# First MLP's weight conversion: ScalarE writes the scaled absolute value into a tile of its own

## The chip, the cores and the metric

The kernel runs on one core of a Trainium2 chip. The core has five instruction queues: TensorE (PE, matrix products), VectorE (DVE), ScalarE (ACT), GpSimd (POOL) and SyncE (SP, which here only issues DMA transfers). Each queue runs its own instructions in the order in which they stand; between queues, an instruction waits for semaphores. The metric is device microseconds (us) of the program. Before the change three runs took 1099.03, 1103.13 and 1106.37 us; their median is 1103.13 us.

## What is computed

Attention with a decay bias over 4 batches, 8 heads, 576 positions and 64 dimensions, and then two MLPs over the 2304 rows of its output, all to nearly float32 exactness. The weights come as float64.

```python
scores = where(causal, -1e9, q @ k.T / 8 + minimum(-(cum[:, None] - cum[None, :]), 0))   # cum = cumsum(relu(s))
attn   = softmax(scores) ; x = attn @ v                    # then (2304, 512)
h = x @ w_in ; g = relu(h) + log1p(exp(-abs(h))) ; x1 = g @ w_out      # first MLP,  512 -> 2048 -> 512
h = x1 @ w_in2 ; g = P(h) / (Q(h) + 1e-6) ; out = g @ w_out2           # second MLP, same sizes
```

## The kernel before

**Products.** Each float32 operand is split into a high part (rounded to the type that PE multiplies at full rate) and a low part (the rest), and a product is three matmuls: high by high, high by low, low by high.

**Tiles.** The first MLP goes over tiles of rows: T0 and T1 of 256 rows each, then four of 448. For each of 16 slices `ff` of the hidden dimension a *unit* multiplies the rows with the slice of `w_in` (`stage_a`, lines 670 to 672, into bank `h`), applies the activation (`stage1`, lines 760 to 764: three ACT instructions and one DVE; `stage3`, lines 800 and 802: high part on ACT, low part on POOL) and multiplies with the slice of `w_out` (`stage_b`, lines 706 to 708, into `acc`). The units run T0 with `ff` 0 to 7, T1 with `ff` 0 to 7, then T0 and T1 in turn for `ff` 8 to 15, then the tiles of 448. Attention is interleaved with the units: scores (L318, L319), softmax (L299 to L315), transposes (L372 to L392) with their split (L362, L363), and the product with `v` (L418 to L430).

**Weights.** The float64 words of the first MLP's weights are loaded as pairs of 32-bit words, 512 KB for each of 32 halves (`load_w`, L519 to L521), and turned into float32 on the chip. This is *a conversion*; it makes a tile `tc` (two buffers), in `conv_t`: POOL makes a zero that has the sign of the high word (L536), ACT scales the high word's absolute value in place (L537), DVE shifts the word that ACT wrote and ORs it to POOL's result (L538), and ORs the top bits of the low word to that (L543). Then `conv_hl` makes the high part `w1h` on ACT (L547) and the low part `w1l` on POOL (L548), and a DMA keeps `w1l` in DRAM. L537 writes the same word that L536 reads, so ACT waits for POOL, and DVE waits for ACT. A loaded buffer is free for the next load when L543 has read it. 7 conversions stand before the first unit, the other 25 beside the units of T0 and T1. From the tiles of 448 rows on none of the first MLP's is left; their `w1l` is loaded back.

**Rows of the activations.** `split_x` (L639 on ACT, L640 on DVE) makes the high and low part of the 512 columns of a tile of rows in four steps `k`, in tiles with the tag `xs`: nine buffers of 128x512 words for the whole kernel. T0 and T1 take four each (high and low share one), a tile of 448 rows two for each `k`.

**Order.** A scheduler writes each engine's order when the program is built, from its own estimate of when operands are ready, priorities (`ahead`, `early`) and some fixed orders (`queue_behind`). An edit of one instruction can so move many others.

Of the kernel before, what the change touches and what calls it, by code (L numbers as in the profile page):

```python
# [8 lines left out]
F32 = mybir.dt.float32  # L9
F32R = mybir.dt.float32r  # L10
I32 = mybir.dt.int32
AF = mybir.ActivationFunctionType
ALU = mybir.AluOpType
# [41 lines left out]
def moe_chain_kernel(ctx, tc, qk0, qk, vv, s0, s, w1, w2, ab, out):  # L55
    nc = tc.nc
    sb = ctx.enter_context(tc.tile_pool(name="sb", bufs=1))
# [466 lines left out]
    def conv(m, ff, half, hi, lo):  # L524
        conv_hl(conv_t(m, ff, half), hi, lo)

    def conv_t(m, ff, half):
        r = raw64.pop((m, ff, half))
        lw = r[:, :, 0]
        hf = r.bitcast(F32)[:, :, 1]  # L530
        hw = r[:, :, 1]
        t = sb.tile([128, 512], F32, tag="tc", bufs=2, name="tc")
        ti = t.bitcast(I32)
        if m == 0:

            nc.gpsimd.tensor_scalar(t, hf, 0.0, 1.0, op0=ALU.mult, op1=ALU.mult)  # L536
            nc.scalar.activation(hf, hf, AF.Abs, scale=2.0 ** -112)  # L537
            nc.vector.scalar_tensor_tensor(ti, hw, 3, ti, op0=ALU.logical_shift_left, op1=ALU.bitwise_or)  # L538
        else:
            nc.gpsimd.tensor_scalar(hf, hf, 2.0 ** -112, 1.0, op0=ALU.mult, op1=ALU.mult)  # L540
            nc.vector.tensor_scalar(ti, hw, 3, None, op0=ALU.logical_shift_left)
            nc.vector.scalar_tensor_tensor(ti, hw, -2147483648, ti, op0=ALU.bitwise_and, op1=ALU.bitwise_or)
        nc.vector.scalar_tensor_tensor(ti, lw, 29, ti, op0=ALU.logical_shift_right, op1=ALU.bitwise_or)  # L543
        return t
# [29 lines left out]
    def conv2_a(ff, half):  # L574
        c2_open.append((ff, half, conv_t(1, ff, half)))
# [476 lines left out]
```

## Time and profile before

| what | value |
|---|---|
| three runs, us | 1099.03, 1103.13, 1106.37 |
| span of the profiled execution, us | 1100.2 |
| busy: PE, DVE, ACT, POOL, us | 1030.3, 825.4, 836.6, 488.2 |
| first matmul of a tile of 448 rows begins at, us | 240.9 |
| PE busy before 241 us, and from 241 to 1100 us | 184.8 of 241, 845.5 of 859 |

The profile gives the span of the profiled execution, from its first to its last instruction, and no other time of it; the span lies between the lowest and the median of the three runs. Rows of the trace name the line of the kernel, the engine, the tile that is written and the tiles read; `[1.97 <-POOL tc L536]` behind a row says that the engine stood idle for 1.97 us before it, until that instruction of POOL. In a table of stretches (windows) the columns are the stretch, its length, and then for PE, PEld (loading of weights into PE), DVE, ACT and POOL the busy time and, in brackets, the number of instructions; then TensorE's granted clock as a share of full speed, the share of the DMA engines' time, and GB/s. In a list of waits each row gives the waiting engine and line, whom it waited for, the sum in us, how often, and the longest.

### The profile page before, as it was taken

The numbers are of one execution on the slowest core, as the hardware profiler recorded it, in microseconds if no ns is written. First come the engines' busy times: TensorE is split into PE (matmuls) and PEld (weight loads), VectorE is DVE, ScalarE is ACT, GpSimd is POOL, SyncE is SP. The second block draws the span as 40 slices with busy tenths as digits, with TensorE's granted clock in tenths as the row PEclk, the third lists the DMA queues.
The fourth block names the chain that finished last, engine by engine and source line by source line (L and its number), as shares of the span: only waits on it lengthen the run. The fifth ranks groups of instructions, "written<-read, shape, count | busy, mean of one in ns | idle before, by whom it ended". The sixth has DMA issues, their size and how long they took to land.

```text
span 1100.2 us, 17835 instructions
## 1 busy us (share of the span) xinstructions
PE 1030.3 (94%) x5732; PEld 926.5 (84%) x5732; DVE 825.4 (75%) x1904; ACT 836.6 (76%) x1767; POOL 488.2 (44%) x543
## 2 busy tenths in 40 slices
PE   3588889889999999999999999899999999999998
PEld 3477778789888888888999998799999999999996
DVE  6898998777888788886556677667777677776765
ACT  6698888878787788777556555688788888888885
POOL 3655576552222122221244676445445455454543
PEclk9999999999999999999999999899999999999999
DMA  6464566466555464432777974401000010000000
GB/s 227 167 221 158 181 222 217 162 205 178 166 160 158 142 205 132 154 94 66 226 235 223 323 280 149 160 1 45 13 30 29 1 58 1 29 30 1 30 1 29
DMA packets 70493, 140.53 MB, mean 128 GB/s; under 512 B 8384, under 2 KB 23904, under 8 KB 70400
## 3 DMA queue, kind: packets, MB, share of 16 engines
q1 hardware_dynamic: 68000, 135.37, 37.5%
q10 hardware_dynamic: 2400, 4.03, 1.5%
q8 instruction: 45, 0.74, 0.3%
q14 instruction: 48, 0.39, 0.1%
HBM read 112.66 MB, written 22.61 MB: 123 GB/s over the span
## 4 chain that ended last, share of the span: by engine, by line
PE 65%; DVE 5%; DMA 3%; ACT 3%; POOL 2%; issue 2%; SPq 0%; POOLq 0%; ACTq 0%; DVEq 0%
PE h L672 6%; PE h L671 6%; PE h L670 6%; PE acc L715 6%; PE acc L714 6%; PE acc L713 6%; PE at L418 3%; PE at L670 3%; PE at L672 3%; PE at L671 3%; PE acc L706 3%; PE acc L707 3%; PE acc L708 3%; PE at L318 2%; DMA raw64x<-in_w_dram 2%
## 5 line engine op out<-in xcount | busy, mean ns | idle before, releaser
L671 PE MATMUL h<-xs,w1h 128*128 128x448 f32 (+1 forms) x352 | 119.9, 341 | 1.4 <-DVE xs L640 1.4
L670 PE MATMUL h<-xs,w1h 128*128 128x448 f32 (+1 forms) x352 | 119.9, 342 | 1.3 <-DVE e L764 1.0
L707 PE MATMUL acc<-gl,w1h 128*128 128x448 f32 (+1 forms) x352 | 119.1, 338 | 1.2 <-POOL gl L802 1.2
L706 PE MATMUL acc<-gh,w1h 128*128 128x448 f32 (+1 forms) x352 | 119.7, 341 | 0.1
L672 PE MATMUL h<-xs,w1l 128*128 128x448 f32 (+1 forms) x352 | 118.8, 338 | 0.2 <-POOL w1l L548 0.2
L708 PE MATMUL acc<-gh,w1l 128*128 128x448 f32 (+1 forms) x352 | 118.4, 336 | 0.0
L715 PE MATMUL acc<-w2h,gl 128*128 128x512 f32 x288 | 113.8, 395 | 0.4 <-POOL gl L802 0.4
L713 PE MATMUL acc<-w2h,gh 128*128 128x512 f32 x288 | 113.8, 395 | 0.4 <-ACT gh L800 0.4
L714 PE MATMUL acc<-w2l,gh 128*128 128x512 f32 x288 | 113.6, 394 | 0.0
L315 POOL TENSOR_SCALAR PA<-PA,stat 128x384 f32<-128x384 f32 (+3 forms) x112 | 69.3, 622 | 97.2 <-DVE stat L314 51.9
L802 POOL TENSOR_TENSOR gl<-PA,gh 128x384 fp32r<-128x384 f32 x96 | 99.4, 1036 | 6.3 <-issue 4.0
L773 POOL TENSOR_TENSOR tc<-tc,e 128x384 f32<-128x384 f32 x48 | 51.7, 1076 | 102.7 <-ACT tc L771 102.7
L315 POOL TENSOR_SCALAR P<-P,stat 128x576 f32<-128x576 f32 x32 | 26.2, 819 | 143.2 <-DVE stat L313 50.7
L363 DVE TENSOR_TENSOR ptl<-at,pth 128x384 fp32r<-128x384 f32 (+2 forms) x108 | 60.7, 569 | 16.3 <-ACT pth L362 15.1
L312 ACT ACTIVATE PA<-PA,stat 128x384 f32<-128x384 f32 (+3 forms) x112 | 63.9, 571 | 10.3 <-DVE stat L299 9.0
L670 PEld LDWEIGHTS h<-xs,w1h 128*128 128x128 f32 x352 | 67.0, 191 | 5.5 <-DVE e L764 1.7
L671 PEld LDWEIGHTS h<-xs,w1h 128*128 128x128 f32 x352 | 66.8, 190 | 5.0 <-DVE xs L640 2.2
L707 PEld LDWEIGHTS acc<-gl,w1h 128*128 128x128 f32 x352 | 66.4, 189 | 4.9 <-POOL gl L802 2.0
L362 ACT ACTIVATE pth<-at 128x384 fp32r<-128x384 f32 (+2 forms) x108 | 53.3, 499 | 21.4 <-PE at L392 12.2
L706 PEld LDWEIGHTS acc<-gh,w1h 128*128 128x128 f32 x352 | 66.4, 189 | 3.6 <-DVE yb L736 0.5
L672 PEld LDWEIGHTS h<-xs,w1l 128*128 128x128 f32 x352 | 66.6, 189 | 3.1 <-POOL w1l L548 0.4
L708 PEld LDWEIGHTS acc<-gh,w1l 128*128 128x128 f32 x352 | 66.2, 188 | 3.0
(225 smaller groups left out, 3311.9 us busy)
## 6 DMA issues: line engine op xcount, KB each, us to landing
w1l<-l_d SPq DMA_DIRECT2D x148, 256.0 KB
raw<-in_w_dram SPq DMA_DIRECT2D x48, 512.0 KB
raw<-in_qk_dram SPq DMA_DIRECT2D x32, 384.0 KB
l_d<-w1l SPq DMA_DIRECT2D x32, 256.0 KB
raw64x<-in_w_dram SPq DMA_DIRECT2D x16, 512.0 KB
R<-in_vv_dram SPq DMA_DIRECT2D x16, 320.0 KB
raw<-in_qk_dram SPq DMA_DIRECT2D x8, 576.0 KB
out_dram<-yb SPq DMA_DIRECT2D x18, 256.0 KB
```

What stands on the lines that cost most here:

```text
L312: nc.scalar.activation(pt[:, 0:n], pt[:, 0:n], AF.Exp, bias=mn, scale=-1.0, accum_out=stat[:, i, 1:2])
L315: nc.gpsimd.tensor_scalar(pt[:, 0:n], pt[:, 0:n], stat[:, i, 2:3], 1.0, op0=ALU.mult, op1=ALU.mult)
L670: nc.tensor.matmul(h, wh[:, cs], xh, start=(k == 0), stop=False)
L671: nc.tensor.matmul(h, wh[:, cs], xl, start=False, stop=False)
L672: nc.tensor.matmul(h, wl[:, cs], xh, start=False, stop=(k == KD - 1))
L706: nc.tensor.matmul(o, wh[:, cs], gh, start=first and not both, stop=False)
L707: nc.tensor.matmul(o, wh[:, cs], gl, start=False, stop=False)
L708: nc.tensor.matmul(o, wl[:, cs], gh, start=False, stop=last and (not both or m % 2 == 1))
L713: nc.tensor.matmul(acc[m], gh[:, cs], wh, start=first, stop=False)
L714: nc.tensor.matmul(acc[m], gh[:, cs], wl, start=False, stop=False)
L715: nc.tensor.matmul(acc[m], gl[:, cs], wh, start=False, stop=last)
L802: eng.tensor_tensor(gl, g, f(gh), op=ALU.subtract)
```

## The change

ACT's instruction writes a tile `xa` of its own, and DVE reads that tile in place of the loaded word. `xa` is taken from the nine `xs` buffers. No instruction is added or removed; line numbers behind it go up by two.

```diff
             nc.gpsimd.tensor_scalar(t, hf, 0.0, 1.0, op0=ALU.mult, op1=ALU.mult)
-            nc.scalar.activation(hf, hf, AF.Abs, scale=2.0 ** -112)
-            nc.vector.scalar_tensor_tensor(ti, hw, 3, ti, op0=ALU.logical_shift_left, op1=ALU.bitwise_or)
+            a = sb.tile([128, 512], F32, tag="xs", bufs=9, name="xa")
+            nc.scalar.activation(a, hf, AF.Abs, scale=2.0 ** -112)
+            nc.vector.scalar_tensor_tensor(
+                ti, a.bitcast(I32), 3, ti, op0=ALU.logical_shift_left, op1=ALU.bitwise_or)
```

The scheduler's order changes on all engines up to the start of the tiles of 448 rows, and hardly behind it. Three places:

ACT, in the attention of the first heads, around the third and fourth conversion (`raw_395`, `raw_397` are their loaded words; `pth` is the high part of a head's transposed probabilities, `gh` the probabilities). Before:

```order
L312 ACTIVATE gh,stat<-gh,stat 128x256 [waits DVE_49]
L537 ACTIVATE raw_395<-raw_395 128x512 [waits DMAHW4_49,Pool_49]
L362 ACTIVATE pth<-acc 128x384 [waits PE_49]
L537 ACTIVATE raw_397<-raw_397 128x512 [waits DMAHW5_49,Pool_49]
L312 ACTIVATE gh,stat<-gh,stat 128x128 [waits DVE_49]
```

With the change:

```order
L538 ACTIVATE xa<-raw_395 128x512 [waits DMAHW4_49]
L312 ACTIVATE gh,stat<-gh,stat 128x128 [waits DVE_49,Pool_49]
L290 ACTIVATE vs<-R 128x5x2x64 [waits DMAHW2_49]
L549 ACTIVATE w1h<-tc 128x512 [waits DVE_49]
L281 ACTIVATE st<-raw 64x576 [waits DMAHW5_49]
L549 ACTIVATE w1h<-tc 128x512 [waits DVE_49,Pool_49]
L312 ACTIVATE gh,stat<-gh,stat 128x256 [waits DVE_49]
L362 ACTIVATE pth<-acc 128x384 [waits PE_49]
L312 ACTIVATE gh,stat<-gh,stat 128x128 [waits DVE_49,Pool_49]
L538 ACTIVATE xa<-raw_397 128x512 [waits DMAHW7_49]
```

The conversion's instruction waits for its load alone, no longer for POOL, and stands further ahead: the third one six rows ahead of the `pth` that it stood directly in front of.

ACT, at the end of T1, behind the last conversion (`xs<-x_277 128x64` and `xs<-x_1873 128x384` are the high parts of one `k` of the first tile of 448 rows). Before, in whose order the first `k` stands more than 100 rows further up:

```order
L537 ACTIVATE raw_2948<-raw_2948 128x512 [waits DMAHW3_49,Pool_49]
L800 ACTIVATE gh<-e 128x256 [waits DVE_49]
L761 ACTIVATE e<-e 128x256 [waits Activation_49]
L290 ACTIVATE vs<-R 128x5x2x64 [waits DMAHW1_49]
L762 ACTIVATE e<-e 128x256 [waits Activation_49]
L547 ACTIVATE w1h<-tc 128x512 [waits DVE_49]
L760 ACTIVATE e<-h 128x256 [waits PE_49,Pool_49]
L639 ACTIVATE xs<-x_277 128x64
L800 ACTIVATE gh<-e 128x256 [waits DVE_49]
L761 ACTIVATE e<-e 128x256 [waits Activation_49]
L639 ACTIVATE xs<-x_1873 128x384
```

With the change:

```order
L538 ACTIVATE xa<-raw_2976 128x512 [waits DMAHW3_49]
L764 ACTIVATE e<-e 128x256 [waits Activation_49]
L762 ACTIVATE e<-h 128x256 [waits PE_49,Pool_49]
L290 ACTIVATE vs<-R 128x5x2x64 [waits DMAHW0_49]
L802 ACTIVATE gh<-e 128x256 [waits DVE_49]
L763 ACTIVATE e<-e 128x256 [waits Activation_49]
L549 ACTIVATE w1h<-tc 128x512 [waits DVE_49]
L764 ACTIVATE e<-e 128x256 [waits Activation_49]
L641 ACTIVATE xs<-x_277 128x64
L641 ACTIVATE xs<-x_1890 128x384
```

All four `k` now stand behind the last conversion, three did before: the ninth buffer, which took the first `k` early, now goes from conversion to conversion.

PE, where attention of the first rows ends and the first unit begins (`at<-ht` and `acc<-ht` are scores of the next rows, `h<-xs,w1h` the first unit). Before:

```order
L318 MATMUL at<-ht 128x384 [waits DVE_49,PE_49,Activation_49]
L319 MATMUL at<-st 128x384 [waits DMAHW4_49]
L418 MATMUL h<-pth,vs_285 128x256 [waits Activation_49]
L418 MATMUL h<-pth,vs_285 128x256
L372 MATMUL acc<-ident,gh 128x128 [waits PE_49,Pool_49]
L372 MATMUL acc<-ident,gh 128x128 x2
L318 MATMUL acc<-ht 128x512 [waits PE_49]
L319 MATMUL acc<-st 128x512
```

With the change:

```order
L418 MATMUL h<-pth,vs_285 128x256 [waits Activation_49]
L418 MATMUL h<-pth,vs_285 128x256
L418 MATMUL h<-ptl,vs_285 128x256 [waits DVE_49]
L418 MATMUL h<-ptl,vs_285 128x256
L672 MATMUL h<-xs,w1h 128x256 [waits PE_49,Activation_49]
L318 MATMUL at<-ht 128x384 [waits DVE_49]
L319 MATMUL at<-st 128x384 [waits DMAHW5_49]
L318 MATMUL acc<-ht 128x512
```

The last head's product with `v` and one matmul of the first unit now stand ahead of the next scores.

## Rows read from the trace of the kernel before

**Rows 1.** The page: span, and busy time with its share and instructions by engine.

```profile
span 1100.2 us, 17835 instructions
PE 1030.3 (94%) x5732; PEld 926.5 (84%) x5732; DVE 825.4 (75%) x1904; ACT 836.6 (76%) x1767; POOL 488.2 (44%) x543
```

**Rows 2.** Windows by stage; columns as told above.

```profile
0.00:57.00 57.00, 27.74 (x103) 22.65 (x103) 42.66 (x128) 37.67 (x88) 29.09 (x46) 1.00 0.59 199
57.00:120.00 63.00, 52.82 (x367) 47.02 (x365) 56.41 (x155) 54.73 (x130) 36.07 (x41) 0.97 0.52 176
120.00:178.00 58.00, 51.02 (x383) 46.71 (x383) 52.93 (x147) 51.53 (x138) 36.49 (x47) 1.00 0.68 223
178.00:241.00 63.00, 53.25 (x417) 50.80 (x416) 49.11 (x116) 50.28 (x128) 39.31 (x45) 1.00 0.56 187
241.00:1100.00 859.00, 845.49 (x4468) 759.32 (x4468) 624.25 (x1360) 642.35 (x1287) 347.26 (x367) 1.00 0.34 109
```

**Rows 3.** Groups by line, 0 to 241 us: count, busy us, mean ns, idle before.

```profile
L538 DVE SCALAR_TENSOR_TENSOR tc<-raw,tc 128x512 int32<-128x512 int32 x32 | 28.1, 880 | 11.3 <-ACT raw L537 11.0
...
L537 ACT ACTIVATE raw<-raw 128x512 f32<-128x512 f32 x32 | 21.5, 675 | 14.1 <-POOL tc L536 14.1
```

**Rows 4.** Timeline, one conversion: start us, us, engine, line, idle before.

```profile
185.58 0.64 POOL L536 TENSOR_SCALAR tc<-raw 128x512 f32<-128x512 f32 x1
186.25 0.69 ACT L537 ACTIVATE raw<-raw 128x512 f32<-128x512 f32 x1 [1.97 <-POOL tc L536]
```

**Rows 5.** Timeline of VectorE, four of the ten L538 between 178 and 241 us.

```profile
186.98 0.69 DVE L538 SCALAR_TENSOR_TENSOR tc<-raw,tc 128x512 int32<-128x512 int32 x1 [1.49 <-ACT raw L537]
...
213.95 0.73 DVE L538 SCALAR_TENSOR_TENSOR tc<-raw,tc 128x512 int32<-128x512 int32 x1 [0.59 <-ACT raw L537]
...
216.87 0.69 DVE L538 SCALAR_TENSOR_TENSOR tc<-raw,tc 128x512 int32<-128x512 int32 x1 [0.65 <-ACT raw L537]
...
234.79 0.69 DVE L538 SCALAR_TENSOR_TENSOR tc<-raw,tc 128x512 int32<-128x512 int32 x1 [2.18 <-ACT raw L537]
```

**Rows 6.** Waits between 178 and 241 us: sum us, times, longest.

```profile
DVE tc L538 <- ACT raw L537: 8.3, 7, 2.2
...
ACT raw L537 <- POOL tc L536: 6.7, 10, 2.0
PE at L318 <- DVE ptl L363: 6.0, 5, 2.2
...
POOL tc L536 <- DMA raw<-in_w_dram: 2.9, 2, 1.7
```

**Rows 7.** Waits between 0 and 57 us.

```profile
ACT raw L537 <- POOL tc L536: 6.4, 5, 1.9
...
DVE tc L538 <- ACT raw L537: 2.8, 2, 1.5
```

**Rows 8.** Timeline: the third conversion on ScalarE, and TensorE behind it.

```profile
36.95 0.66 ACT L537 ACTIVATE raw<-raw 128x512 f32<-128x512 f32 x1 [1.93 <-POOL tc L536]
37.52 0.47 ACT L362 ACTIVATE pth<-acc 128x384 fp32r<-128x384 f32 x1
...
38.04 0.80 PE L418 MATMUL acc<-pth,vs 128*128 128x256 f32 x2 [2.94 <-ACT pth L362]
```

**Rows 9.** Waits between 120 and 178 us.

```profile
ACT raw L537 <- POOL tc L536: 1.2, 2, 1.0
```

**Rows 10.** Timeline of ScalarE: the first `k` of the first 448-row tile.

```profile
174.40 0.27 ACT L639 ACTIVATE xs<-x 128x64 fp32r<-128x64 f32 x1
...
174.88 0.51 ACT L639 ACTIVATE xs<-x 128x384 fp32r<-128x384 f32 x1
```

**Rows 11.** Timeline of TensorE: first matmul of the 448-row tiles.

```profile
240.89 0.47 PE L670 MATMUL h<-xs,w1h 128*128 128x448 f32 x1 [0.18 <-DVE e L764]
```

**Rows 12.** Timeline: an L538 beside GpSimd's two-input subtraction.

```profile
45.32 1.28 POOL L548 TENSOR_TENSOR w1l<-tc,w1h 128x512 fp32r<-128x512 f32 x1
...
45.63 1.51 DVE L538 SCALAR_TENSOR_TENSOR tc<-raw,tc 128x512 int32<-128x512 int32 x1 [1.24 <-ACT raw L537]
```

## The prediction

> **What bounds the kernel now.** The page comes first: PE is busy for 1030.3 of 1100.2 us [rows 1], so at most 70 us are to be had without shortening PE's own work. The windows by stage tell where they lie [rows 2]. From 241 us on PE is busy for 845.5 of 859 us, and no conversion of the first MLP is left there: what the change does must show as an earlier or later start of the tiles of 448 rows, whose first matmul now begins at 240.89 us [rows 11]. Ahead of it PE lacks 241 − 184.8 = 56.2 us: 29.3 in the start (0 to 57), 10.2 and 7.0 in the middle (57 to 120, 120 to 178), 9.8 at the end of T0 and T1 (178 to 241). In the middle DVE is busy for 56.41 of 63 and 52.93 of 58 us, ACT hardly less; so there these two set the pace, with 90% and no long stops. At both ends they have room: 42.66 of 57 and 49.11 of 63 us for DVE [rows 2].
>
> Next, who stops them there. Over the 32 conversions ACT stands for 14.1 us before L537, always for POOL, and DVE for 11.0 us before L538, for ACT [rows 3]. One conversion shows how: POOL ends at 186.22, ACT, which has stood for 1.97 us, runs from 186.25 to 186.94, and DVE, which has stood for 1.49, begins at 186.98 [rows 4, 5]. The three are strictly in a row. By stage: in the start ACT stands for 6.4 us and DVE for 2.8 [rows 7], at the end of T0 and T1 for 6.7 and 8.3 [rows 6], in the middle ACT for 1.2 and in the first half of it not at all [rows 9]; 6.4 + 1.2 + 6.7 is the 14.1, with one stop of 0.2 at 178 us that both stretches count. That DVE's stops reach PE is seen in the same list: PE waits 6.0 us for L363, a DVE instruction that stands in the queue behind L538 [rows 6].
>
> **The change part by part.** No instruction is added, and the two changed ones keep their sizes: 0.69 us on ACT, 0.69 on DVE when nothing disturbs it [rows 4, 5]. What is removed is ACT's wait for POOL; DVE now waits for both. Behind the load, POOL and ACT can run side by side, so a conversion's chain gets shorter by ACT's part.
>
> *End of T0 and T1.* DVE waits for ACT seven times, 8.3 us in all [rows 6]. Of a wait of over 0.69 us only ACT's 0.69 goes, since POOL's end, 0.69 earlier, is late next; a shorter one goes whole. Two are shorter, 0.59 and 0.65; five are longer, from 1.07 to the 2.18 at 234.79 [rows 5]. Sum: 5 × 0.69 + 0.59 + 0.65 = 4.7 us. From below it is 0 (the time is taken by the next load: POOL waited 2.9 us for two of them [rows 6]; but a load starts when L543 has read its buffer, and L543 comes earlier too); from above 8.3, if the scheduler's new order makes POOL earlier as well. I take 4.7, all of it on the path, because PE's 6.0 us behind L363 are larger.
>
> *Start.* ACT's stop holds what is queued behind it: after 1.93 us before L537 comes L362, for which PE then waits 2.94 [rows 8]. In the new order the conversions no longer stand in between with a wait for POOL. DVE's direct loss is 2.8 us, ACT's stop 6.4 [rows 7]. The value lies between 0 (PE's waits of the start go to other releasers, whose chain is not touched) and 6.4. I take 2.8, the wait on the busier engine. PE's moved scores cost nothing in this sum: the last head ends earlier by about what its product was moved ahead.
>
> *Middle.* DVE is 90% busy and loses nothing to L537 there; 0, at most the 1.2 of ACT [rows 9].
>
> *The buffers.* `xa` comes from the nine `xs` buffers. When T1's four are taken, eight are held to the end of T0 and T1, and the last 16 conversions share one: ACT's instruction then waits for the DVE instruction of the conversion before. That costs nothing while two conversions are further apart than one takes; the closest above begin at 213.95 and 216.87, 2.9 us apart [rows 5], against 1.4 for ACT and DVE together. Its upper bound is the 6.7 us that ACT stands now [rows 6]. But the ninth buffer also served the first `k` of the first 448-row tile, whose two ACT instructions ran at 174 us, 0.27 and 0.51 us [rows 10]. In the new order they stand behind the last conversion, where PE's next tile waits for the splits: +0.8 us.
>
> *Contention.* L538 takes 0.69 us undisturbed, but 0.88 in the mean [rows 3, 5]: 32 × 0.19 = 6 us go to those that run beside POOL, as the one of 1.51 us beside L548 [rows 12]. DVE now starts when POOL starts its next instruction, so more of them may. By the row, an L539 beside a subtraction would take 1.51; by the mean, 0.88. I keep 0.88, because POOL's next subtraction often has to wait for ACT anyway; the other end is a rival. The Trainium skill (GPSIMD Engine Reference, 8. Key points) says that GpSimd shares its SBUF interfaces with VectorE and contends with VectorE instructions that have two inputs in SBUF; L538 and L539 are of that kind, and the row of 1.51 us agrees. By that rule the gain would be smaller or turn into a loss; by the undisturbed row it stays.
>
> **Sum:** −4.7 − 2.8 + 0.8 = −6.7 us. Against the profiled execution: span 1100.2 − 6.7 = 1093.5 us [rows 1]. The median of the three runs, 1103.13, is 2.9 above that span; 1103.1 − 6.7 = **1096.4 us**, 0.6% less.
>
> **The rivals.**
> 1. *All of ACT's stops come back.* ACT's 14.1 us [rows 3] free the whole queue, and DVE and PE behind it, and nothing else comes late: 1103.1 − 14.1 = 1089.0 us. For it: PE lacks 29.3 us in the start and 9.8 at the end [rows 2], so there is room. Against it: only 8.3 and 2.8 of these stops reach DVE now.
> 2. *The wait only changes its name.* DVE waits for POOL as long as it did for ACT, since POOL itself waits in its queue, the last 16 ACT instructions wait for the shared buffer, and what is won in the start is lost in the middle, where DVE's work is unchanged and sets the pace. Then only the 0.8 us stay: 1103.9 us. For it: 90% in the middle [rows 2], and POOL's waits for loads [rows 6].
> 3. *Contention takes more than it gave (slower).* Each L539 runs beside a subtraction of POOL and takes 1.51 instead of 0.88 us: 32 × 0.63 = 20 us more of DVE. With all of it on the path, 1096.4 + 20 = 1116.5 us. The point from which it is a loss is a mean of L539 of 0.88 + 6.7 / 32 = 1.09 us; slower by 1% it is from 1.43 on. Against it: three of the four rows shown have 0.69 [rows 5], and POOL runs 39 of 63 us there [rows 2], not all of them subtractions.
>
> **How the numbers follow.** The forecast gets 0.45, with 1090 to 1101 as its own range (upper bounds of both ends, 8.3 + 6.4 with some of it lost; lower bounds near 0); the first rival 0.25, the second 0.18, the third 0.12. A measurement of this kernel tells about 1% (11 us) from no change. Under 1092.1 us come the first rival and a tenth of the forecast: 0.29. Over 1114.2 comes most of the third: 0.10. Within 1%: 0.61. The range that leaves out 2 in 10 goes from 1085 us, past the first rival, to 1109, about half of the way to the third.
>
> **What would show it.** Right: in the new trace ACT does not wait before L538 for POOL, neither in the start nor at the end; DVE's wait before L539 is on POOL, and its sum at the end of T0 and T1 is near 8.3 − 4.7 = 3.6 us; L539's mean is near 0.88; the first matmul of a tile of 448 rows begins at about 234 us, and what comes behind it takes the same 859 us. The start: the first matmul of the first unit comes some 3 us earlier. Wrong: ACT waits on DVE before L538 with several us (the shared buffer); L539's mean over 1.1 (contention); DVE busier in the middle than 90% with the same start of the 448-row tiles (second rival); or PE waiting for the first unit's `xs` ahead of scores that stood ready.

## The result and the profile after

The change made the kernel slower: 1109.46 us against 1102.28 us, both medians of six runs, ratio 1.0064 with a 95% interval of 1.0047 to 1.0081. That is +7.2 us where −6.7 was forecast. It is less than the 1% that the prediction took as the least that can be told from no change, but the interval leaves no doubt about the sign.

The page of the changed kernel, the counterpart of [rows 1]:

```profile
span 1107.2 us, 17845 instructions
PE 1034.8 (93%) x5732; PEld 935.3 (84%) x5732; DVE 828.3 (75%) x1904; ACT 837.5 (76%) x1767; POOL 491.3 (44%) x543
```

The windows by stage of the changed kernel, with the columns of [rows 2] (length, then busy time and count of PE, PEld, DVE, ACT and POOL, granted clock, DMA share, GB/s):

```profile
0.00:57.00 57.00, 27.80 (x102) 22.07 (x102) 42.83 (x120) 37.57 (x87) 27.78 (x45) 0.70 0.60 195
57.00:120.00 63.00, 49.88 (x329) 46.31 (x329) 53.64 (x143) 50.32 (x118) 36.06 (x37) 0.89 0.59 190
120.00:178.00 58.00, 49.20 (x366) 45.92 (x364) 52.28 (x151) 48.24 (x128) 33.90 (x41) 0.97 0.58 188
178.00:241.00 63.00, 54.03 (x399) 52.35 (x398) 51.16 (x121) 50.23 (x127) 41.70 (x48) 0.92 0.55 181
241.00:1107.00 866.00, 853.93 (x4546) 768.62 (x4544) 628.40 (x1372) 651.12 (x1310) 351.86 (x374) 1.00 0.35 110
```

The loss is in the middle. From 57 to 120 us PE, DVE and ACT are all busy for less than before (49.88, 53.64 and 50.32 us against 52.82, 56.41 and 54.73): no engine has become the bound, all three wait more. So the tiles of 448 rows start late. Their first matmul, the counterpart of [rows 11], in the timeline of TensorE (start, duration):

```profile
250.30 0.36 PE L672 MATMUL h<-xs,w1h 128*128 128x448 f32 x1
```

That is 9.4 us later than the 240.89 of before, and ScalarE's first evacuation of T0 says the same: 262.51 us (L726) against 253.46 (L724). What follows takes 1107.2 − 250.3 = 856.9 us, 2.4 less than the 859.3 of before. 9.4 − 2.4 = 7.0 us is the difference of the spans. (Every time of a first 448-column matmul here and below is from one profiled execution, so a difference of one or two us between two kernels is not firm.)

The waits that the change was about are gone, and others have come. Groups by line over 0 to 241 us (count, busy us, mean ns, idle time before and its releaser), the counterparts of [rows 3]; the last group is the softmax's exponential on ScalarE:

```profile
L539 DVE SCALAR_TENSOR_TENSOR tc<-xa,tc 128x512 int32<-128x512 int32 x31 | 29.6, 958 | 10.2 <-POOL tc L536 7.6 <-ACT xa L538 2.3
L312 ACT ACTIVATE PA<-PA,stat 128x384 f32<-128x384 f32 (+3 forms) x42 | 24.1, 575 | 13.0 <-DVE stat L299 13.0
L538 ACT ACTIVATE xa<-raw 128x512 f32<-128x512 f32 x31 | 20.5, 664 | 0.0
```

ScalarE no longer stands for 14.1 us before the conversion, but for 0.0. Instead it stands for 13.0 us before L312, for VectorE's L299, a wait that came to 1.9 us before. VectorE's stop before the conversion has kept its size (11.3 us before, 10.2 now, with one conversion behind 241 us) and only changed its releaser, from ACT to POOL. By stage, the waits from 178 to 241 us (sum, times, longest), the counterparts of [rows 6]:

```profile
PE at L318 <- DVE ptl L363: 7.2, 4, 2.6
DVE tc L539 <- POOL tc L536: 4.3, 4, 2.1
...
POOL tc L536 <- DMA raw<-in_w_dram: 1.2, 1, 1.2
DVE tc L539 <- ACT xa L538: 0.9, 1, 0.9
```

And from 0 to 57 us, the counterpart of [rows 7]:

```profile
DVE tc L539 <- POOL tc L536: 3.3, 3, 1.4
```

At the end of T0 and T1 VectorE's 8.3 us have become 5.2; in the start its 2.8 us for ACT have become 3.3 for POOL.

**How far attention has come** is seen in the rows of L312 by stretch (two rows for each softmax, the exponential and the reading of its sum). Before:

```profile
0.00:57.00 57.00, 9.22 (x36) 1.00 0.59 199
57.00:140.00 83.00, 19.97 (x54) 0.98 0.54 180
140.00:178.00 38.00, 5.75 (x20) 1.00 0.72 240
178.00:241.00 63.00, 7.54 (x24) 1.00 0.56 187
```

After:

```profile
0.00:57.00 57.00, 7.82 (x32) 0.70 0.60 195
57.00:140.00 83.00, 18.03 (x46) 0.90 0.57 183
140.00:178.00 38.00, 7.74 (x28) 1.00 0.62 202
178.00:241.00 63.00, 9.14 (x30) 0.92 0.55 181
```

At 140 us 90 rows had run before and 78 now: six softmaxes behind, though the changed kernel has by then done no more units and no more conversions. The first of the late rows stand around 55 us. The timeline of VectorE before (the last column is idle time and its releaser):

```profile
51.35 0.55 DVE L299 CUSTOM_DVE_ANT_0 PA<-at,mask 128x384 f32<-128x384 f32 x1
...
53.23 0.69 DVE L299 CUSTOM_DVE_ANT_0 PA<-acc,mask 128x512 f32<-128x512 f32 x1 [1.32 <-PE acc L319]
...
55.33 0.68 DVE L538 SCALAR_TENSOR_TENSOR tc<-raw,tc 128x512 int32<-128x512 int32 x1
```

The same stretch after:

```profile
52.92 0.86 DVE L642 TENSOR_TENSOR xs<-x,xs 128x256 fp32r<-128x256 f32 x1 [0.56 <-ACT xs L641]
...
55.60 1.14 DVE L539 SCALAR_TENSOR_TENSOR tc<-xa,tc 128x512 int32<-128x512 int32 x1 [1.36 <-POOL tc L536]
56.77 0.56 DVE L299 CUSTOM_DVE_ANT_0 PA<-at,mask 128x384 f32<-128x384 f32 x1
...
57.86 0.68 DVE L299 CUSTOM_DVE_ANT_0 PA<-acc,mask 128x512 f32<-128x512 f32 x1
```

Two softmax rows that stood ahead of a conversion now stand behind one, and behind its wait of 1.36 us for POOL; they come 5.4 and 4.6 us later. Most of the first delay comes from TensorE, where the scores that the first row reads now stand behind the last head's product and a matmul of the first unit. Before:

```profile
48.86 0.53 PE L319 MATMUL at<-st 68*128 68x384 f32 x1
```

After:

```profile
53.64 0.52 PE L319 MATMUL at<-st 68*128 68x384 f32 x1
```

That is 4.8 of the 5.4 us; the scores of the second row come 1.8 us later (54.38 against 52.56), and the rest is VectorE's. ScalarE waits for the two rows, with the next conversion and a `w1h` queued behind (its timeline after):

```profile
57.44 0.61 ACT L312 ACTIVATE PA<-PA,stat 128x384 f32<-128x384 f32 x1 [1.90 <-DVE stat L299]
...
58.05 0.65 ACT L538 ACTIVATE xa<-raw 128x512 f32<-128x512 f32 x1
58.61 0.61 ACT L549 ACTIVATE w1h<-tc 128x512 fp32r<-128x512 f32 x1
```

The Trainium skill (Perfetto Trace Analysis, Tensor Engine Instruction (MATMUL, LD_WEIGHTS)) says that ScalarE, VectorE and GpSimd are strictly first in, first out; the row agrees, since L538 starts only behind L312, although no wait is shown before it. Whether these two late rows make the loss is taken up at e7 and e8: by themselves they don't.

### The profile page after: what moved, and what is told of

It is laid out like the page before. It is cut to its first block, busy times and chain, and to the rows that moved or that the text cites. A ratio compares the mean times of both kernels' runs of the same rounds, so it can differ in the third digit from the quotient of the medians.

```text
span 1107.2 us, 17845 instructions
## 1 busy us (share of the span) xinstructions
PE 1034.8 (93%) x5732; PEld 935.3 (84%) x5732; DVE 828.3 (75%) x1904; ACT 837.5 (76%) x1767; POOL 491.3 (44%) x543
## 4 chain that ended last, share of the span: by engine, by line
PE 70%; DVE 10%; ACT 6%; POOL 5%; issue 5%; DMA 4%; SPq 0%; POOLq 0%; ACTq 0%; DVEq 0%
PE h L673 6%; PE h L674 6%; PE h L672 6%; PE acc L717 6%; PE acc L716 6%; PE acc L715 6%; PE at L418 4%; PE acc L708 3%; PE acc L709 3%; PE acc L710 3%; PE at L672 3%; PE at L674 3%; PE at L673 3%; PE at L318 3%; PE at L319 2%
## 5 line engine op out<-in xcount | busy, mean ns | idle before, releaser
L312 ACT ACTIVATE PA<-PA,stat 128x384 f32<-128x384 f32 (+3 forms) x112 | 64.0, 571 | 21.1 <-DVE stat L299 20.3
L363 DVE TENSOR_TENSOR ptl<-at,pth 128x384 fp32r<-128x384 f32 (+2 forms) x108 | 60.8, 569 | 17.0 <-ACT pth L362 15.4
L673 PEld LDWEIGHTS h<-xs,w1h 128*128 128x128 f32 x352 | 68.2, 194 | 5.5 <-DVE xs L642 2.3
L672 PEld LDWEIGHTS h<-xs,w1h 128*128 128x128 f32 x352 | 68.1, 194 | 4.5 <-ACT xs L641 0.8
```

What stands on the lines that cost most here:

```text
L312: nc.scalar.activation(pt[:, 0:n], pt[:, 0:n], AF.Exp, bias=mn, scale=-1.0, accum_out=stat[:, i, 1:2])
L672: nc.tensor.matmul(h, wh[:, cs], xh, start=(k == 0), stop=False)
L673: nc.tensor.matmul(h, wh[:, cs], xl, start=False, stop=False)
```

## The experiments

All runs are of whole kernels, and each ratio is to runs of the kernel before on the same chip. Four theories stand against each other. **A**: the scheduler, seeing ScalarE's instruction ready earlier, writes another order, and that order costs the time; the buffer by itself gains a little. **B**: the new instruction itself costs, by contention between DVE's L539 and POOL. **C**: the difference is TensorE's granted clock, 0.995 in the mean before and 0.969 after. **D**: the buffer taken from the splits is missed there.

To separate order and buffer, an order is held with dependencies that put no semaphore in (`after`, which the kernel already uses for its start): a table names, for each engine, its instructions in the order of another built kernel.

```diff
+        em = list(nc.cur_bb.bb.instructions)
+        for seq in pinned_order().values():
+            for i, j in zip(seq, seq[1:]):
+                after(em[j], em[i])
```

| run | conversion | `xs` buffers | order | ratio to before, 95% | first 448-column matmul, us |
|---|---|---|---|---|---|
| before | in place | 9 | scheduler's | 1 | 240.89 |
| after | `xa` from `xs` | 9 | scheduler's | 1.0064 (1.0047 to 1.0081) | 250.30 |
| e1 | in place | 9 | after's, held | 1.0097 (1.0081 to 1.0112) | 252.82 |
| e2 | `xa` own tag | 8 | e3's, held | 0.9943 (0.9928 to 0.9959) | 242.09 |
| e3 | in place | 8 | scheduler's | 0.9946 (0.9932 to 0.9960) | 243.80 |
| e4 | `xa` own tag | 8 | scheduler's | 1.0004 (0.9992 to 1.0017) | 249.25 |
| e5 | `xa` own tag | 8 | start of e3, rest free | 0.9937 (0.9924 to 0.9949) | 240.16 |
| e6 | `xa` own tag | 8 | e3's to 120 us, rest free | 0.9956 (0.9941 to 0.9971) | 243.86 |
| e7 | in place | 9 | priority 49 | 1.0013 (1.0004 to 1.0022) | 243.18 |
| e8 | in place | 9 | priority 60 | 1.0004 (0.9993 to 1.0015) | 241.40 |
| e9 | `xa` own tag | 8 | start of e4, rest of e3 | 0.9969 (0.9959 to 0.9979) | 245.13 |
| e10 | in place | 9 | start of after, rest free | 1.0022 (1.0010 to 1.0034) | 243.88 |
| e11 | in place | 8 | start of e4, rest free | 1.0009 (0.9998 to 1.0020) | 247.70 |
| e12 | in place | 9 | its own, held | 1.0001 (0.9991 to 1.0012) | 240.82 |

### The control

e12 adds the lines above to the kernel before, with the table of its own order.

> A control: the kernel before with every engine's instructions held by order-only dependencies in its own order. If holding an order costs nothing in itself, 0.999 to 1.001, first 448-column matmul at 240 to 242 us; if the device costs something, e1, e2, e5, e6 and e9 are to be read with that much taken off.

Measured 1.0001. Holding an order costs nothing that can be seen (by the interval at most 1.3 us), so the other runs can be read as they stand.

### e1: the old conversion in the new order

The lines above in the kernel before, with the table of the changed kernel; ScalarE's 32 absolute values are left out of it.

> The kernel before, conversion in place as it was, with every engine's instructions held by order-only dependencies (no semaphores) in the order that the changed kernel has; only ScalarE's 32 absolute values may stand where they become ready, since in that order they could not wait for GpSimd. Theory A (the new order of the instructions costs the time, the new buffer itself gains a little): slower than before by at least the 7.2 us of the changed kernel, ratio 1.006 to 1.015, first 448-column matmul at 248 to 256 us, and the waits of ScalarE before L312 for VectorE's L299 are about 13 us in the first 241 us, as in the changed kernel. Theory B (contention: the new buffer costs, whatever the order): as before, ratio 0.998 to 1.002, first 448-column matmul at 240 to 242 us. Theory C (TensorE's granted clock): the time follows the mean granted clock of the run, and the order makes no difference at the same clock.

Measured 1.0097, first 448-column matmul at 252.82 us. Its waits from 0 to 241 us:

```profile
ACT raw L537 <- POOL tc L536: 18.2, 15, 2.6
DVE tc L538 <- ACT raw L537: 14.3, 13, 2.8
ACT PA L312 <- DVE stat L299: 6.2, 12, 1.3
```

The order alone, with not one buffer of the program changed, puts off the start of the 448-row tiles by 11.9 us, more than the whole change. Part of this is paid by the old conversion itself, which waits more in that order: ScalarE 18.2 us for POOL where it was 14.1, VectorE 14.3 for ScalarE where it was 11.0. B and C do not ask for that. ScalarE's wait for L299 came out at 6.2 us, not at 13: part of it may be taken over by the stops before L537, which stand in the same queue. The new buffer then gives back 252.82 − 250.30 = 2.5 us. So the two halves of the change have opposite signs, and the order is the larger.

### e2 and e3: the new conversion in the old order

e3 is one number:

```diff
-        return sb.tile(shape, F32R, tag="xs", bufs=9, name="xs")
+        return sb.tile(shape, F32R, tag="xs", bufs=8, name="xs")
```

e2 is the changed kernel with that line, a tag of its own for `xa` (one buffer, the diff is at e4), and the table of e3's order without ScalarE's absolute values.

> The kernel before with 8 instead of 9 buffers for the splits of x, nothing else: what it costs that one buffer is taken from the splits, and the partner of e2. Theory A: the first 448-column matmul moves by under 1 us, since the order up to there hardly changes; the later tiles may lose some us because the next tile's first split comes later, ratio 1.000 to 1.008. If the buffer taken from the splits were the cause of the changed kernel's loss (theory D), the first 448-column matmul would come 7 to 9 us later here too.

> The other half: the new conversion, its absolute value in a buffer of a tag of its own (1 buffer, the tag of the splits 8 instead of 9), with every engine held in the order of the kernel e3, which is that of the kernel before as far as 8 buffers allow; only ScalarE's absolute values are free. To be read against e3. Theory A: the waits go and nothing takes their place: 3 to 7 us less than e3, ratio to e3 0.994 to 0.997, ScalarE waits under 1 us for GpSimd before L538, first 448-column matmul 3 to 7 us earlier than in e3. Theory B: slower than e3 by 2 to 5 us, with L539 at a mean of 0.95 us or more. Theory C: no difference but that of the clock.

Measured: e3 0.9946, e2 0.9943. The waits from 178 to 244 us of e3:

```profile
POOL tc L536 <- DMA raw<-in_w_dram: 7.9, 6, 3.5
DVE tc L538 <- ACT raw L537: 6.3, 4, 3.9
ACT raw L537 <- POOL tc L536: 4.7, 4, 3.7
```

and of e2:

```profile
POOL tc L536 <- DMA raw<-in_w_dram: 4.7, 6, 1.3
DVE tc L539 <- ACT xa L538: 1.2, 2, 1.1
DVE tc L539 <- POOL tc L536: 0.8, 2, 0.5
```

With the order kept, the waits fall as predicted: VectorE's from 6.3 to 2.0 us, that is −4.3 where −4.7 was forecast. But only 1.7 us of that reach the first 448-column matmul (242.09 against 243.80), and next to nothing the end (0.9943 against 0.9946, where theory A had 3 to 7 us). They are gone by the end of T5, the last tile of 448 rows: its evacuation starts at 695.0 us in e2 and 694.8 in e3, with 254.38 and 256.31 for T0's. There the conversions of the second MLP stand on DVE, and in e2 PE waits for it between 614 and 697 us, as it does not in e3:

```profile
PE h L672 <- DVE e L766: 1.3, 1, 1.3
```

B is out for this order: L539 takes 883 ns in e2 and L538 876 in e3, in the mean. Nor does the time follow that mean elsewhere: L538 takes 805 ns in e10 and 803 in e11, which are slower than before and than e3, and L539 921 ns in e6, which is faster than before.

That e3 is 5.9 us faster than before was not expected, and its 448 columns start 2.9 us *later* (its last conversions wait longer for their loads, 7.9 against 2.9 us). The gain is at the other end of the program, where the second MLP begins. ScalarE splits its first rows there; before, in the timeline of ScalarE, this stands for 5.04 us:

```profile
690.88 0.53 ACT L643 ACTIVATE yt<-yt 128x384 fp32r<-128x384 f32 x1 [5.04 <-DMA w2h<-w_d]
```

and PE behind it:

```profile
700.50 0.69 PE L670 MATMUL h<-yt,w2h 128*128 128x384 f32 x1 [4.50 <-DVE PA L775]
```

In e3 the same instruction stands for 0.57 us, and PE has no such stop:

```profile
692.02 0.53 ACT L645 ACTIVATE yt<-yt 128x384 fp32r<-128x384 f32 x1 [0.57 <-DMA yt<-y_d]
```

So this gain has nothing to do with the conversion: it lies some 450 us behind the last conversion of the first MLP. Nor does it come with one order or another: it goes with the number of buffers. In the traces of all seven kernels with nine `xs` buffers (before, after, e1, e7, e8, e10, e12) ScalarE's split stands there for 4.2 to 5.7 us and PE has a stop of 4.4 to 4.5; in all seven with eight (e2 to e6, e9, e11) the split stands for 0.5 to 1.6 us and PE has no such stop. From the first 448-column matmul to the end the nine-buffer kernels take 856.7 to 859.3 us, the eight-buffer kernels 850.7 to 854.3. How one buffer less takes the wait away is not shown. So totals are compared below between kernels with the same number of buffers. D is wrong in sign.

### e4: the new conversion with a tag of its own, order free

e2 without the table; against the changed kernel:

```diff
-            a = sb.tile([128, 512], F32, tag="xs", bufs=9, name="xa")
+            a = sb.tile([128, 512], F32, tag="xa", bufs=1, name="xa")
...
-        return sb.tile(shape, F32R, tag="xs", bufs=9, name="xs")
+        return sb.tile(shape, F32R, tag="xs", bufs=8, name="xs")
```

> The changed kernel with its absolute value in a buffer of a tag of its own (1 buffer; the splits have 8), and the order left to the scheduler. In the changed kernel the first unit's splits stand behind eight conversions, since tiles of one tag are handed out in the program's order; here they stand ahead of them again, but the rest of the order is new too. Theory A': the shared tag alone put the order wrong: 1092 to 1101 us at a median of before of 1102, first 448-column matmul at 234 to 240 us. Theory A with any new order worse than the tuned one: 1102 to 1110 us, 448 columns from 242 us on. Theory B: 1105 to 1110 with L539 at 0.95 us or more.

Measured 1.0004, first 448-column matmul at 249.25 us. In the changed kernel ScalarE's first split for the first unit stands behind seven conversions (the text above says eight), at 52.48 us, since tiles of one tag are handed out in the program's order; before, it ran at 20.68. With the tag of its own it is back at 20.37 us, and the 448 columns still start late. So up to there the shared tag is worth about 1 us; theory A' falls, and A stays. That the whole time is nearly that of before, and not that of the changed kernel, is in the main the gain of the eight buffers at the second MLP. Against e3 the freed order costs 0.0058, 6.4 us.

### e5 and e6: how much of the old order is needed

e2 with a shorter table, and whatever is not in it behind the table's last instruction on its engine:

```diff
+        ends = {em[q[-1]].engine: (em[q[-1]], set(q)) for q in pinned_order().values()}
+        for n, i in enumerate(em):
+            if i.engine in ends and n not in ends[i.engine][1] and ...
+                after(i, ends[i.engine][0])
```

> As e2 (new conversion, own buffer, 8 buffers for the splits), but only the first instructions of every engine, up to the 103rd matmul (what the kernel before has issued at 57 us), are held in the old order; behind them the scheduler orders freely. e4 (nothing held) took 1103.0 us and e2 (everything held) 1095.9 us. If the new order loses in the start (conversions 5 to 7 ahead of the attention rows that the kernel before has there), this run keeps most of e2's gain: 1094 to 1098 us, first 448-column matmul at 241 to 244 us. If it loses in the middle, 57 to 140 us, it is as e4: 1101 to 1105 us, 448 columns from 247 us on. By the theory of the TensorE clock the time goes with the mean clock alone.

> As e5, but held up to the 470th matmul (120 us in the kernel before). If start and middle carry the loss: 1094 to 1098 us, as e2, whatever the scheduler orders behind. If the order behind 120 us matters too: between e2 and e4, 1098 to 1102 us.

Measured: e5 0.9937, e6 0.9956, first 448-column matmuls at 240.16 and 243.86 us. The old start alone brings back all that e4 lost against e2, though the rest is ordered as freely as in e4. The rows of L312 in e5 up to 140 us:

```profile
0.00:57.00 57.00, 9.12 (x36) 1.00 0.58 197
57.00:140.00 83.00, 20.06 (x54) 0.96 0.55 180
```

36 and 54, as before.

### e7 and e8: is any other order worse?

A push to the scheduler's priorities, nothing else; e8 has 60 in place of 49.

```diff
-C1_OFF = 50
+C1_OFF = 49
```

> The kernel before with C1_OFF = 49 in place of 50, one step of the scheduler's priority for the conversions, no buffer and no wait changed: only the order of the instructions changes. If the old order is one that a small push loses (theory A in its general form: nearly any other order is worse), 1105 to 1113 us, first 448-column matmul at 246 to 253 us. If orders are about equal and the new conversion's own reordering is special, 1099 to 1104 us.

> The same with C1_OFF = 60, a second push in the other direction. Expected as in e7: 1105 to 1113 us if nearly any other order is worse, 1099 to 1104 us if not.

Measured 1.0013 and 1.0004. A step of one in a priority does reorder every engine and moves the 448 columns by 2.3 us, but it costs 1.4 us at the end, not 3 to 11. So it is not so that nearly any other order is worse; the order that the new conversion brought is a bad one among those tried.

These two runs also bear on the late softmax rows around 55 us. In both, the two rows stand directly behind a conversion on VectorE and come as late as in the changed kernel; in the timeline of VectorE of e8:

```profile
57.19 0.54 DVE L299 CUSTOM_DVE_ANT_0 PA<-at,mask 128x384 f32<-128x384 f32 x1
```

Yet e8 begins its 448 columns at 241.40 us. So these late rows alone don't cost the time. What tells the orders apart comes behind them: of L312's rows 32 have run at 57 us in the changed kernel, in e1, e4 and in e7 to e11, but at 140 us 76 in e1, 78 in the changed kernel, 79 in e11, 83 in e10, 84 in e4, e7 and e9, and 86 in e8, where before has 90. Roughly, the fewer there are, the later the 448 columns begin; e4, with 84 rows and 249.25 us, is the exception.

### e9, e10 and e11: is it the start alone?

e9 has e4's order up to the 103rd matmul and e3's behind it; e10 and e11 hold the starts of the changed kernel and of e4 in kernels with the old conversion (before and e3). The lines are those of e1 (e9) and e5 (e10, e11); only the tables differ.

> The complement of e5: new conversion with its own buffer, every engine's first instructions (up to the 103rd matmul) in the order that the scheduler gave e4, all others in the old order among themselves, as in e2. With e2 (old start, old rest: 0.9943 of before), e5 (old start, free rest: 0.9937) and e4 (new start, free rest: 1.0004) it closes the square. If the start's order alone makes the loss: 0.999 to 1.003, first 448-column matmul from 247 us on. If the loss is what the scheduler makes of the rest behind a new start: 0.994 to 0.997, 448 columns at 242 to 245 us.

> The kernel before with its conversion in place and 9 buffers; only the first instructions (up to the 103rd matmul) are held in the order of the changed kernel, the rest is free. If the start's order costs whatever the conversion is: slower than before by 5 to 11 us, ratio 1.004 to 1.010, first 448-column matmul from 246 us on. If it costs only together with the new conversion or the order behind it: 0.999 to 1.003.

> As e3 (old conversion, 8 buffers), with the start held in the order of e4 and the rest free: against e4 (1.0004) it differs by the conversion alone, as far as the free rest allows, and against e3 (0.9946) by the start's order. If the start's order costs: 0.999 to 1.005, first 448-column matmul from 247 us on. If not: 0.994 to 0.997.

Measured 0.9969, 1.0022 and 1.0009. For the conversion with its own buffer the square is:

| | rest in the old order | rest free |
|---|---|---|
| old start | e2 0.9943 | e5 0.9937 |
| new start | e9 0.9969 | e4 1.0004 |

The new start costs 0.0026 (2.9 us) with the old rest and 0.0067 (7.4 us) with the free one. e9 lies at the upper edge of the second of its two ranges, with its 448 columns at 245.13 us just outside, and under the first: neither reading was right alone. The start's order costs some 3 us by itself, and the scheduler then makes of the rest an order that costs about as much again. e10 says the same for the old conversion: the changed kernel's start alone costs 0.0022, 2.4 us (the smaller of its two ranges, not the 5 to 11 us of the other), and with the rest as in e1 0.0097. e11 against e4 (1.0009 and 1.0004, the same start, old and new conversion) shows once more that the buffer by itself is worth next to nothing.

C is out too: e3 has a mean granted clock of 0.980 and is faster than before with 0.995; e10 has 0.991 and is slower. In the 82 runs of the kernel before that stand beside the experiments, the 34 with a clock of 0.988 or more took 1102.2 us in the mean and the 48 with 0.981 or less 1102.0. The matmuls themselves give little: from 57 to 120 us the 84 of `h<-xs` took 310 ns in the mean after and the 91 before 296, in all some 1.2 us.

What stays open: which of the moved instructions costs how much, and by what chain the start's order sets back the stretch from 57 to 140 us. Attention's rows show the lag; e7 and e8 rule out the two late rows at 55 us as its whole cause, and no other instruction was moved by itself.

## Why the prediction was wrong

- **What bounds the kernel**: right. The loss lies ahead of the tiles of 448 rows (+9.4 us, where about −7 was forecast); from their first matmul on these take 856.9 us, where 859 was given.
- **ScalarE no longer waits for POOL**: right, 0.0 us. **No wait for the shared buffer**: right; no stop before L538 is shown.
- **End of T0 and T1, −4.7**: the mechanism was right and its size nearly so, but only with the order kept (−4.3 in e2 against e3); in the changed kernel VectorE's 8.3 us fall to 5.2, not to 3.6. The step that failed is "all of it on the path": 1.7 of 4.3 us reached the 448-row tiles, and next to nothing the end. Its ground was misread. PE's 6.0 us behind L363 were taken as VectorE's stops before the conversion, but the longest of these waits ends behind an L363 that had itself waited for ScalarE. In the changed kernel PE's wait for L363 is 7.2 us, though VectorE's stops are shorter. The two lines, of VectorE and TensorE before:

```profile
197.50 0.56 DVE L363 TENSOR_TENSOR ptl<-at,pth 128x384 fp32r<-128x384 f32 x1 [1.33 <-ACT pth L362]
198.11 0.45 PE L318 MATMUL at<-ht 128*128 128x384 f32 x1 [2.21 <-DVE ptl L363]
```

- **Start, −2.8**: failed. The first matmul of the first unit came earlier as foretold (52.94 us against 55.17), but then PE waited 1.4 us for the unit's next `xs` (VectorE's L642), the kind of wait that the prediction had named as a sign against it. VectorE's wait was not taken away, it got POOL as its releaser (3.3 us); the second rival had said so. PE's wait, in its timeline after:

```profile
59.01 0.39 PE L673 MATMUL h<-xs,w1h 128*128 128x256 f32 x1 [1.41 <-DVE xs L642]
```

- **Middle, 0**: this is where the sum went wrong. It asked what each removed wait was worth at its place, and took the order around it as given, though the rows of the order ahead of the prediction showed that all engines had been rearranged. "PE's moved scores cost nothing" priced one of those moves by itself (the last head's product did end 4.2 us earlier, and the scores came 4.8 us later); the others got no price. The step that failed is this: a term for the new order was put at nothing without a reason. It measured +11.9 us with the old conversion (e1), and +7.2 us with the new one in its own buffer (249.25 in e4 against 242.09 in e2); the buffer's own term in the changed kernel's order is −2.5.
- **Buffers, +0.8**: the first 448-column matmul had no wait for a split, so this was not seen. The shared tag had another effect that was not foreseen, the late split of the first unit (52.48 us), which is worth about 1 us up to the 448-row tiles by e4.
- **Contention kept at 0.88**: nearly right. L539's mean is 0.96 us after, under the 1.09 from which it would have turned the sum; 0.08 × 32 = 2.6 us, and in the old order nothing (883 against 876 ns). The Trainium skill's rule on the shared interfaces (GPSIMD Engine Reference, 8. Key points) agrees with the longer L539 in sign, but is not the cause: with the old conversion the new order is slower still.
- **The rivals**: the one on the slower side had the right sign for a wrong reason. None of them was "the scheduler answers with a worse order", which the rows of the order allowed, and the range ended at 1109 us, just under the result.

The version to keep is e3 or e5: 1096.1 and 1096.0 us, where before has 1102. e3 is one number, and it leaves the conversion as it was; what it gains, it gains at the second MLP.

## What to carry to other kernels

Where a scheduler writes the order, an edit of one wait is two edits: the wait, and the new order. Price them apart: hold the old order with dependencies that carry no semaphore, which cost nothing that could be seen here (e12), and see what the wait is worth there; then let the order go. Don't put the new order at nothing where several engines are 85 to 90% busy: here the lag grew in such a stretch, on all engines at once. And before blaming the instructions that are seen to be late, look for a run that has them just as late without the loss; here e7 and e8 did. A change of one buffer can also act far from where it was made: compare totals only between kernels with the same number. And push a priority by one before taking a gain of under 1% for the edit's own: with the same instructions and buffers, before and e1 lie 10.7 us apart by their order alone.

## What the runs showed of the hardware

The granted clock on record for a stretch need not be the one that its matmuls ran at. Between 40 and 57 us the record has 1.00 before and 0.50 in e3, the two levels of 2.4 and 1.2 GHz, in nearly the same order of instructions, with PE busy for about 60% of the stretch. The windows, of before:

```profile
40.00:57.00 17.00, 10.72 (x38) 8.59 (x38) 13.14 (x37) 11.44 (x29) 10.98 (x14) 1.00 0.61 201
```

and of e3:

```profile
40.00:57.00 17.00, 10.50 (x37) 8.35 (x38) 13.13 (x38) 11.51 (x30) 10.97 (x14) 0.50 0.62 200
```

Yet the matmuls took the same time. The groups by shape from 38 to 57 us, of before:

```profile
L671 PE MATMUL h<-xs,w1h 128*128 128x256 f32 x2 | 0.8, 415 | 0.0
```

and of e3:

```profile
L673 PE MATMUL h<-xs,w1h 128*128 128x256 f32 x2 | 0.8, 415 | 0.0
```

The same form takes 284 ns in the mean between 120 and 178 us of before. The starts say the same: the first three matmuls of the unit begin 0.21 us apart in both (55.17, 55.39 and 55.60 us before; 55.40, 55.62 and 55.83 in e3), and three of before from 57.92 us on 0.12 us apart. So both ran slowly in the start, whatever the record says, and the lower mean clock of the changed kernel's page is by itself no proof that its matmuls ran slower. The Trainium skill (TensorE: Matmul & The Clock Gate, Seeing it yourself) warns that the clock's events in a trace can be unreliable; these rows agree.
